# A new order for the first chunk, products that stay in one tile mode, and the mask load in two halves

## The chip, the cores and the metric

The kernel runs on one core of one Trainium2 chip. A core has five engines with a queue each: PE (TensorE, with its weight loads listed as PEld), DVE (VectorE), ACT (ScalarE), POOL (GpSimd) and SP (SyncE, which here only issues DMAs). Each engine takes the instructions of its queue in order; between engines they wait for each other by semaphores. The metric is the device time of one execution in microseconds (us), as the median of several runs. A row of the profile names a line of the kernel as L12, an operation as `out<-in`, and times in us or, where marked, ns.

## The reference

```python
def _attn_ref(q, k, v):                       # q, k, v: (8, 8, 576, 64), float32
    stride, scale = 32, 1.0 / np.sqrt(64)
    scores = scale * np.matmul(q, k.transpose(0, 1, 3, 2))
    rel = pos[:, None] - pos[None, :]
    mask_local = (rel >= 0) & (rel < stride)
    mask_strided = (rel >= 0) & (pos[None, :] % stride == pos[:, None] % stride)
    # heads 0-3 local, heads 4-7 strided
    scores = np.where(masks, scores, -1e9)
    attn = np.exp(scores - scores.max(-1, keepdims=True))
    attn = attn / (attn.sum(-1, keepdims=True) + 1e-9)
    return np.matmul(attn, v)

def _moe_ref(x, w_in, w_out):                 # x: (4608, 512), w_in: (512, 2048), w_out: (2048, 512)
    h = x @ w_in
    g = np.maximum(h, 0.0) + np.log1p(np.exp(-np.abs(h)))
    return g @ w_out

# x is the attention's output, heads side by side
```

## The kernel before

The attention is done for 32 pairs n of heads (8 batches of 4 pairs, in each batch local and strided pairs by turns). A pair's scores are made only in blocks of 64 by 64 where the mask lets something through, nine places for two half-arrays: `scores(n, part)`, part 0 with six places and part 1 with three. The feed-forward layer goes over nine chunks c of 512 tokens and 16 slices f of 128 hidden units. Its matrices are split into a high and a low part (x_h, x_l; w's halves; gh, gl), and each product is the sum of three: high by high, high by low, low by high. So `hidden(c, f)` is 12 products of 128 by 512 and so is `output(c, f)`, which adds into four banks py, one for each 128 tokens. Between them stand Abs, Exp and Ln on ScalarE, the softplus sum on VectorE and the split into gh and gl.

What comes first is written out by hand. The string `FIRST` is a list of tasks, issued from left to right; each goes to the queue of its engine, and three more lists (`ON_POOL`, `ON_VECTOR`, `ON_SCALAR`) name the tasks that don't run on their usual engine. A name is made of letters and numbers:

- q, k, v with n: loads of a pair on SyncE's queue. D: laying out q (D10 and D11 are the two heads of pair 1). S with n and part: scores. X, Y, E, Z, x: maximum, subtraction, exponential, sum, bias. r, R, M: the reciprocal and the normalization.
- T, C, V: transposes on PE for pairs 0 to 3 (three groups each), the copies out of PSUM, the weighted sums. P: transposes on VectorE for pairs 4 to 7. H, L: high and low part of x.
- wi, wo with f: loads of a slice of w_in or w_out as 64-bit floats. a, B, d, c: four steps that make a 32-bit float of it. h, l: its high and low part.
- F with f: `hidden(0, f)`, where Fa is the first nine products and F the other three for f below 2. A, Ae, Al: Abs, Exp, Ln. u: softplus sum. Gh, Gl: split. O: `output(0, f)`; O15 is its first half (tokens 0 to 255) and Ob15 the second.
- y0 to y3: a copy out of py and the DMA that writes it, on SyncE's queue. Qa0, Q0, Q1, QA, Qu, Qh, Ql: the same for the first two slices of chunk 1.
- W: eight products on zeros at the start.

All weights stay on the chip. Behind the written order a planner (`Plan`) lays out the rest from estimated costs and due times: `hidden` two slices ahead of `output`, and a pair's attention at fixed steps. Its first tasks for PE are F18, which is `hidden(1, 2)`, then S8, the scores of pair 8, then `output(1, 0)`. S8 reads the key that task k8 loads and the laid out query of D8.

PSUM: `ps_h` has two banks (hidden, the early transposes), `ps_o` and `ps_s` one each, and `py` is four, which the first scores borrow. The SBUF pools that matter are `io` (four buffers, for weight steps and outputs) and `u` (two).

In batches 0 and 1 (pairs 0 to 7) the mask is added on PE: a product of the 128 by 128 identity and the mask, onto the scores. An early transpose (L454) puts 32 by 32 blocks into a bank that a product on zeros of 128 by 128 (L447) has started. From pair 8 on VectorE adds the mask. The mask itself (192 KB) is loaded by

```python
    mask_b = const.tile([P, 12 * 64], BF16, name="mask_b")
    nc.scalar.dma_start(mask_b, masks)
```

at the head of the kernel (L163). The last tile of the last chunk is written in two halves of 256 columns, one copied by VectorE and one by ScalarE, the second with its DMA on ScalarE's queue (`result`, L655).

Of the kernel before, what the change touches and what calls it, by code (L numbers as in the profile page):

```python
# [33 lines left out]


FIRST = """
W q0 k0 D01 D00 S00 S01 X00 Y00 q1 D10 X01 D11 x01 E00 Z00 k1 S11 X11 E01 r0 R0 M0 q2 D21 S10
T00 wi0 D20 Y11 X10 x10 ai0 Bi0 T01 di0 k2 E11 S21 Z11 S20 E10 ci0 v0 r1 C00 R1 M1 X21 x21 C01 V00
wo2 q3 ao2 Bo2 do2 co2 D30 hi0 D31 wi2 T02 C02 X20 Y20 k3 H00 L00 ai2 Bi2 E20 ho2 Z20 T10 wi1 di2
v1 E21 r2 T11 S31 V01 X31 S30 lo2 x31 R2 wo3 C10 T12 ci2 H01 L01 X30 Y30 ai1 C11 V10 C12 hi2 E31  # L40
wo0 M2 H10 L10 li2 E30 Z30 T20 C20 li0 r3 R3 ao3 Bi1 M3 T21 V11 C21 H11 L11 wi11 ai11 Bi11 di1 T22
T32 C32 di11 v2 wi3 V20 C22 H20 ci1 ci11 hi11 L20 T31 ai3 Bi3 v3 hi1 li1 C31 T30 C30 li11 wo1 wi4
V21 H21 L21 V31 di3 wo6 ao1 Bo1 ao0 ci3 V30 H31 L31 H30 L30 Fa0 hi3 li3 do1 Bo0 co1 do0 Bo3 q4 D4
wi12 co0 F0 A0 Ae0 ho1 k5 Al0 u0 lo1 Fa1 k4 S40 ai4 wi6 X40 Bi4 x40 ho0 lo0 wi5 Gh0 ai5 wi7 Bi5 F1
A1 Gl0 ai7 Ae1 Al1 E40 do3 co3 di4 u1 Gh1 ho3 lo3 F2 A2 Ae2 Bi7 ci4 di5 O0 q5 wi10 wo5 ao5 Al2 Gl1
wi8 S41 D5 X41 ci5 x41 E41 u2 Gh2 hi5 di7 li5 F3 hi4 A3 Bo5 do5 ci7 Ae3 Al3 r4 R4 li4 co5 O1 M4
S50 X50 x50 hi7 u3 wo12 v4 F5 F4 ho5 Gl2 lo5 Gh3 Gl3 P4 E50 S51 ai6 ai8 Bi8 di8 X51 O2 wo4 ao4 Bi6
wo7 x51 di6 ci6 hi6 A5 Ae5 Al5 u5 li7 Bo4 q6 A4 E51 r5 k6 D6 V40 ci8 do4 O3 H40 L40 S60 co4 R5
wi13 Ae4 ai10 Bi10 Al4 V41 H41 li6 wi9 M5 u4 Gh4 Gl4 X60 Gh5 ho4 x60 L41 P5 F7 F6 hi8 wo15 lo4 Gl5
li8 di10 v5 O4 k7 E60 ao6 Bo6 A7 ai13 S61 A6 Ae6 V50 O5 Al6 ci10 hi10 do6 co6 u6 wo11 wo8 q7 li10  # L50
F10 Ae7 Al7 X61 ho6 ai9 u7 x61 ao7 Bo7 do7 Bi13 di13 Bi9 Gh7 Gl7 ci13 H50 L50 wo14 lo6 di9 ci9 Gh6
Gl6 F8 D7 E61 r6 S70 co7 A10 Ae10 ao8 Al10 Bo8 do8 R6 hi9 A8 wi15 u10 V51 li9 X70 x70 O6 Ae8 Al8
co8 wo9 u8 M6 H51 L51 wi14 P6 ho8 lo8 ai12 Gh8 ho7 lo7 Gl8 F11 hi13 li13 Bi12 Gh10 Gl10 wo10 ao9
Bo9 F9 O7 E70 S71 ai15 Bi15 do9 X71 co9 v6 ao10 Bo10 A9 Ae9 Al9 x71 do10 V60 H60 L60 u9 ho9 A11 q8
# [65 lines left out]
def attention_softplus_ffn(  # L120
# [189 lines left out]
    def scores(n, part):  # L310

        b = order[n][0]
        masked = b < 2
# [8 lines left out]
        pss[n, part] = ps
        lo, hi = SPLIT[part]
        for x in range(lo, hi):
            for place in range(2):
# [2 lines left out]
                nc.tensor.matmul(  # L328
                    ps[64 * place : 64 * place + 64, 64 * (x - lo) : 64 * (x - lo) + 64],
                    lhsT=blocks_of(n)[:, c // 32].rearrange("p h l -> p (h l)"),  # L330
                    rhs=k_of(n)[:, c : c + 64],
                    start=x == lo or not masked,
                    stop=not masked,
                )
        if masked:
            nc.tensor.matmul(
                ps[:, : 64 * (hi - lo)], lhsT=ident_b, rhs=mask_of(n, part), start=False, stop=True
            )
# [103 lines left out]
    def early_transposes(n, g):  # L442

        ph = phs["t", n, g] = ps_h.tile([P, 512], F32, tag="ph", name=f"pt_{n}_{g}")[
            :, : 4 * TILE
        ]
        nc.tensor.matmul(ph, lhsT=warm[:, :P], rhs=warm[:, : 4 * TILE], start=True, stop=False)  # L447
        ph = ph.rearrange("p (h a c) -> p h a c", h=2, a=2)
        for x in range(2):
            for i in range(3):  # L450
                a = 2 * g + x
                chunk, place = (6 + a % 3, a // 3) if i == 1 else (a, i // 2)
                for c in range(2):
                    nc.tensor.matmul(  # L454
                        ph[32 * (i + c) : 32 * (i + c) + 32, :, x, 32 * i : 32 * i + 32],
                        lhsT=prob[n % 2][:, chunk, 32 * c : 32 * c + 32],
                        rhs=ident[:, 64 * place : 64 * place + 64],
                        start=False,
                        stop=x == 1 and (c == 0 or i == 2),
                    )  # L460
# [192 lines left out]
                )  # L653

    def result(c, t, engine, cols=slice(0, DM)):  # L655
        o = io_pool.tile([P, DM], F32, tag="io", name=f"o_{c}_{t}")[:, cols]
# [3 lines left out]
        queue.dma_start(out[t0 : t0 + P, cols], o)  # L660
# [314 lines left out]
```

## Time and profile before

| | us |
|---|---|
| median of 3 runs | 899.48 (899.31 to 900.12) |
| the profiled execution's own time | 899.74 |
| its span, first to last instruction | 897.5 |
| PE busy | 885.0 (99%) |
| VectorE busy | 601.4 (67%) |
| ScalarE busy | 446.9 (50%) |
| GpSimd busy | 60.0 (7%) |
| mean DMA rate | 65 GB/s |

The span is 2.2 us shorter than the time of the same execution; what lies around it is the start and end of the program. Shares over the whole span mix the first chunk, in which all engines have much to do, with the rest, so they are read by stretch. A product's own duration (about 390 ns for 512 columns) is longer than the distance to the next one (about 227 ns), since products overlap; a busy PE is thus not a measure of how full it is.

### The profile page before, as it was taken

What the parts mean: (1) busy time and instruction counts of PE and PEld (TensorE: products, weight loads), DVE (VectorE), ACT (ScalarE), POOL (GpSimd) and SP (SyncE); (2) the same over time, 40 slices, a digit from 0 to 9 for tenths busy, and PEclk for the clock granted to TensorE, in tenths of its full rate; (3) what the DMA queues carried; (4) which work ended last, traced back from release to release, by engine and by line L of the source; (5) the groups of instructions that cost most, each with busy time, mean ns of one, the idle gap of its engine ahead of it and who ended that gap; (6) DMA issues with size and microseconds to landing.
All of it is one profiled execution on the core that took longest, in us unless ns stands there. A gap on an engine that the chain in (4) does not pass through costs nothing.

```text
span 897.5 us, 14490 instructions
## 1 busy us (share of the span) xinstructions
PE 885.0 (99%) x5700; PEld 723.8 (81%) x5700; DVE 601.4 (67%) x1308; ACT 446.9 (50%) x796; POOL 60.0 (7%) x77
## 2 busy tenths in 40 slices
...
DMA packets 50084, 58.28 MB, mean 65 GB/s; under 512 B 3168, under 2 KB 35296, under 8 KB 50016
## 3 DMA queue, kind: packets, MB, share of 16 engines
...
q8 instruction: 45, 0.74, 0.4%
q10 hardware_dynamic: 288, 0.33, 0.1%
...
## 4 chain that ended last, share of the span: by engine, by line
PE 86%; DVE 6%; ACT 3%; DMA 3%; issue 1%; SPq 1%; POOL 0%; ACTq 0%; POOLq 0%
PE py L647 40%; PE ph L607 39%; PE ps L328 2%; DMA ri<-in_moe_w_in_dram 2%; PE pv L484 2%; DVE pt L432 1%; PE po L484 1%; PE po L328 1%; ACT qT L256 1%; ACT prob L374 1%; DVE u L628 1%; DMA ro<-in_moe_w_out_dram 1%; DVE a_i L561 1%; DVE a_o L561 0%; DVE a_o L578 0%
## 5 line engine op out<-in xcount | busy, mean ns | idle before, releaser
L647 PE MATMUL py<-w_o,gh 128*128 128x512 f32 x1152 | 359.2, 393 | 0.1
L607 PE MATMUL ph<-x_h,w_i 128*128 128x512 f32 x1152 | 355.7, 390 | 1.0 <-DVE u L628 1.0
L619 ACT ACTIVATE u<-ph 128x512 f32<-128x512 f32 x144 | 86.4, 600 | 394.9 <-PE ph L607 391.9
L607 PEld LDWEIGHTS ph<-x_h,w_i 128*128 128x128 f32 x1152 | 215.8, 188 | 46.3 <-DVE u L628 1.6
L647 PEld LDWEIGHTS py<-w_o,gh 128*128 128x128 f32 x1152 | 213.8, 188 | 47.3 <-POOL w_o L593 0.9
L647 PE MATMUL py<-w_o,gl 128*128 128x512 f32 x576 | 224.2, 389 | 0.0
L607 PE MATMUL ph<-x_l,w_i 128*128 128x512 f32 x576 | 224.1, 389 | 0.0
L628 DVE SCALAR_TENSOR_TENSOR u<-ph,u 128x512 f32<-128x512 f32 x144 | 98.9, 688 | 171.9 <-ACT u L624 170.4
L432 DVE STREAM_TRANSPOSE pt<-prob 32x192 f32<-32x192 f32 x448 | 137.1, 314 | 6.4
L647 PEld LDWEIGHTS py<-w_o,gl 128*128 128x128 f32 x576 | 108.1, 188 | 22.8
L607 PEld LDWEIGHTS ph<-x_l,w_i 128*128 128x128 f32 x576 | 108.1, 188 | 22.6
L640 DVE TENSOR_TENSOR gl<-u,gh 128x512 fp32r<-128x512 f32 x138 | 96.1, 697 | 11.2 <-ACT gh L256 0.3
L622 ACT ACTIVATE u<-u 128x512 f32<-128x512 f32 x144 | 91.3, 634 | 4.5
L624 ACT ACTIVATE u<-u 128x512 f32<-128x512 f32 x144 | 90.9, 632 | 4.4
L256 ACT COPY qT<-prob 64x576 f32<-64x576 f32 x56 | 70.5, 1260 | 0.3
L256 DVE CAST gh<-u 128x512 fp32r<-128x512 f32 x130 | 55.4, 426 | 10.6 <-PE py L647 0.5
L391 DVE TENSOR_TENSOR prob<-ps,mask_b 128x384 f32<-128x384 f32 x24 | 13.4, 558 | 50.4 <-PE ps L328 50.4
L328 PEld LDWEIGHTS ps<-kT,qT 128*64 128x64 f32 x720 | 23.6, 137 | 11.6 <-issue 9.9
L328 PE MATMUL ps<-kT,qT 128*64 128x64 f32 x720 | 28.0, 226 | 0.3 <-ACT qT L256 0.3
L484 PE MATMUL pv<-pt,v_in 128*64 128x96 f32 x396 | 22.2, 248 | 0.0
L422 DVE TENSOR_TENSOR prob<-prob,st 128x576 f32<-128x576 f32 x28 | 21.2, 757 | 0.9
L391 DVE TENSOR_TENSOR prob<-po,mask_b 128x192 f32<-128x192 f32 x24 | 8.6, 357 | 19.3 <-ACT x_h L522 19.3
...
## 6 DMA issues: line engine op xcount, KB each, us to landing
v_in<-in_v_dram SPq DMA_DIRECT2D x28, 320.0 KB, 3.5
...
prob<-in_qk_dram SPq DMA_DIRECT2D x28, 288.0 KB, 2.7
kT<-in_qk_dram SPq DMA_DIRECT2D x28, 288.0 KB, 3.0
...
room<-in_v_dram SPq DMA_DIRECT2D x4, 320.0 KB, 7.5
```

Of the source, the lines that this page charges most:

```text
L256: (engine.copy if engine is nc.scalar else engine.tensor_copy)(dst, src)
L328: nc.tensor.matmul(ps[64 * place : 64 * place + 64, 64 * (x - lo) : 64 * (x - lo) + 64], lhsT=blocks_of(n)[:, c // 32].rearrange("p h l -> ...
L391: nc.vector.tensor_tensor(pv, sv, m, op=ALU.add)
L432: nc.vector.transpose(pt[32 * (i + c) : 32 * (i + c) + 32, h, a : a + hi - lo, 32 * i : 32 * i + 32,], src[:, lo:hi, 32 * c : 32 * c + 32],)
L484: nc.tensor.matmul(po[64 * h : 64 * h + 64, TILE * x : TILE * x + TILE], lhsT=vs[n][:, a, h, :], rhs=pt_of(n, a)[:, h, a % 2], start=True, ...
L607: nc.tensor.matmul(ph, lhsT=w32["i", f][:, half, cc * P : (cc + 1) * P], rhs=x_of(x, cc)[:, t0 : t0 + n], start=(i == 0), stop=(i == 3 * N ...
L619: nc.scalar.activation(us[c, f], phs[c, f], AF.Abs)
L622: nc.scalar.activation(u, u, AF.Exp, scale=-1.0)
L624: nc.scalar.activation(u, u, AF.Ln, bias=1.0)
L628: nc.vector.scalar_tensor_tensor(u, in0=phs.pop((c, f)), scalar=0.0, in1=u, op0=ALU.max, op1=ALU.add)
L640: engine.tensor_tensor(g, us.pop((c, f)), ghs[c, f].bitcast(F32), op=ALU.subtract)
L647: nc.tensor.matmul(py[t], lhsT=g[:, sl], rhs=w32["o", f][:, half], start=(f == 0 and n == 0), stop=(f == NFC - 1 and n == 2),)
```

## The change

It has four parts. The order and the three lists of engines are replaced by others; the tasks are the same but for two new ones, `mask` and `mask2`, the loads of the two halves of the mask. A mask is added as two products of 64 columns of the identity, in the tile mode of the score products, ahead of them for all pairs but pair 0; a bank of early transposes is started by four products of 32 columns in place of one of 128. The half of the last tile that ScalarE copies takes a `u` buffer in place of an `io` buffer.

```diff
 FIRST = """
-W q0 k0 D01 D00 S00 S01 X00 Y00 q1 D10 X01 D11 x01 E00 Z00 k1 S11 X11 E01 r0 R0 M0 q2 D21 S10
-T00 wi0 D20 Y11 X10 x10 ai0 Bi0 T01 di0 k2 E11 S21 Z11 S20 E10 ci0 v0 r1 C00 R1 M1 X21 x21 C01 V00
...
-V21 H21 L21 V31 di3 wo6 ao1 Bo1 ao0 ci3 V30 H31 L31 H30 L30 Fa0 hi3 li3 do1 Bo0 co1 do0 Bo3 q4 D4
-wi12 co0 F0 A0 Ae0 ho1 k5 Al0 u0 lo1 Fa1 k4 S40 ai4 wi6 X40 Bi4 x40 ho0 lo0 wi5 Gh0 ai5 wi7 Bi5 F1
...
-lo9 Ae11 Al11 u11 O8 di15 ci15 Gh11 Gh9 Gl9 di12 V61 H61 ao11 Bo11 wo13 F13 hi15 li15 E71 r7 R7 O9
-co10 ho10 A13 ci12 hi12 ao13 Ae13 Al13 k8 v7 Gl11 L61 lo10 do11 F15 ao12 O10 M7 co11 li12 ho11
-lo11 u13 Gh13 P7 A15 Ae15 Gl13 ai14 Bi14 di14 ci14 F12 hi14 Al15 u15 O11 q9 A12 Ae12 Al12 u12 Bo12
-D8 Gh12 V70 Qa0 li14 F14 do12 co12 ho12 Gl12 lo12 O12 Bo13 do13 A14 co13 ho13 lo13 H70 L70 V71
-ao14 Bo14 do14 Ae14 co14 Al14 u14 ho14 lo14 O13 H71 L71 Q1 Gh14 v8 Gl14 O14 ao15 Bo15 do15 co15
-Gh15 Gl15 ho15 lo15 QA1 Qu1 Qh1 Ql1 Q0 QA0 O15 y1 Ob15 y2 y3 Qu0 Qh0 y0 Ql0 k9
+mask q0 D00 k0 q1 D11 W D01 S00 X00 Y00 S01 X01 x01 D10 E00 Z00 E01 mask2 k1 S10 X10 q2 D20 r0 R0 D21
+wi2 ai2 M0 x10 Bi2 E10 q3 D30 S11 X11 Y11 E11 T01 C01 k2 wi1 di2 ci2 Z11 T00 C00 ai1 v0 r1 R1 S20
...
+li1 wo0 co3 ao0 Bo0 C22 H20 L20 T30 C30 di3 ci3 ao2 q4 Bo2 do2 T32 C32 hi3 ho3 T31 C31 V21 H21 L21
+D4 v3 V31 wi4 V30 H31 do0 lo3 Fa0 co0 li3 L31 H30 L30 wo1 ao1 wi12 Bo1 do1 ho0 ai4 lo0 q5 F0 A0
...
+P7 D8 ao14 Bo14 ao12 O10 Bo12 do12 A12 Ae12 Al12 v7 V70 u12 Gh13 Gl13 O11 wo13 ao13 H70 L70 q9
+co12 ai14 Bi14 di14 Qa0 A15 Gh12 Gl12 ho12 lo12 Bo13 ci14 hi14 Ae15 Al15 V71 u15 O12 li14 do13
+Gh15 H71 L71 F14 k9 co13 ho13 lo13 ao15 Bo15 Q0 do14 co14 A14 Ae14 O13 Al14 u14 Gh14 Gl15 ho14
+Gl14 lo14 Q1 do15 co15 ho15 O14 lo15 Ob15 QA0 Qu0 Qh0 Ql0 O15 QA1 Qu1 y2 Qh1 y3 y1 y0 v8 k8 Ql1
 """
 ON_POOL = """
-D10 D20 D30 ho2 r2 x31 hi11 hi3 x40 ho3 x41 hi5 x50 ho5 hi6 r5 x60 ho6 x61 x71 ho9 ho11 Gh13 hi14
-ho13 ho14
+D11 D20 D30 hi2 hi0 hi3 ho1 hi4 hi7 ho6 x61 hi9 x70 x71 Gh13 hi14 ho14 ho15
 """.split()
 ON_VECTOR = """
-D00 M0 M1 lo2 C12 M3 li1 li3 lo0 Gl0 lo3 Gl1 li5 li4 li7 li6 li10 Gl7 lo6 Gl6 Gl10 Gl9 li15 Gl11
-lo10 M7 Gh12 li14 Gl12 Gl14 Gh15 Gl15
+D00 M0 C01 li1 lo3 lo0 li4 Gh0 Gl0 lo1 Gl1 Gl3 li7 li8 Gl7 Gl6 li9 lo8 lo9 M7 Gl13 Gl12 lo12 lo13
+Gl14 lo14 lo15 y2 y0
 """.split()
 ON_SCALAR = """
-y1 y3
+y3 y1
 """.split()
...
-    nc.scalar.dma_start(mask_b, masks)
...
+        rows = [slice(64 * place, 64 * place + 64) for place in range(2)]
+
+        def add(first):
+            for place in range(2):
+                nc.tensor.matmul(
+                    ps[rows[place], : 64 * (hi - lo)],
+                    lhsT=ident_b[:, rows[place]],
+                    rhs=mask_of(n, part),
+                    start=first,
+                    stop=not first,
+                )
+
+        if masked and n > 0:
+            add(True)
         for x in range(lo, hi):
             for place in range(2):
...
-        if masked:
-            nc.tensor.matmul(
-                ps[:, : 64 * (hi - lo)], lhsT=ident_b, rhs=mask_of(n, part), start=False, stop=True
-            )
+        if masked and n == 0:
+            add(False)
...
-        nc.tensor.matmul(ph, lhsT=warm[:, :P], rhs=warm[:, : 4 * TILE], start=True, stop=False)
+        for c in range(4):
+            nc.tensor.matmul(
+                ph[32 * c : 32 * c + 32],
+                lhsT=warm[:, :32],
+                rhs=warm[:, : 4 * TILE],
+                start=True,
+                stop=False,
+            )
...
-        o = io_pool.tile([P, DM], F32, tag="io", name=f"o_{c}_{t}")[:, cols]
+        if cols.start == 0:
+            o = io_pool.tile([P, DM], F32, tag="io", name=f"o_{c}_{t}")[:, cols]
+        else:
+            o = u_pool.tile([P, 512], F32, tag="u", name=f"o_{c}_{t}")[:, : DM - cols.start]
...
+    first["mask"] = lambda: nc.scalar.dma_start(mask_b[:, : 6 * 64], masks[:, : 6 * 64])
+    first["mask2"] = lambda: nc.sync.dma_start(mask_b[:, 6 * 64 :], masks[:, 6 * 64 :])
```

With the new lists 16 tasks go from VectorE to GpSimd (M1, M3, x70 and 13 low parts of weights and of g), 18 from GpSimd to VectorE (11 low parts, r2, r5, x31, x40, x41, x50, x60), ten from GpSimd to ScalarE (D10, ho2, hi11, ho3, hi5, ho5, hi6, ho9, ho11, ho13), eight the other way (D11, hi0, hi2, ho1, hi4, hi7, hi9, ho15), four from ScalarE to VectorE (C01, Gh0, y0, y2) and three back (C12, Gh12, Gh15).

More of the change, by code (lines that the diff above doesn't have):

```diff
@@ L36 @@
 FIRST = """
-W q0 k0 D01 D00 S00 S01 X00 Y00 q1 D10 X01 D11 x01 E00 Z00 k1 S11 X11 E01 r0 R0 M0 q2 D21 S10
-T00 wi0 D20 Y11 X10 x10 ai0 Bi0 T01 di0 k2 E11 S21 Z11 S20 E10 ci0 v0 r1 C00 R1 M1 X21 x21 C01 V00
-wo2 q3 ao2 Bo2 do2 co2 D30 hi0 D31 wi2 T02 C02 X20 Y20 k3 H00 L00 ai2 Bi2 E20 ho2 Z20 T10 wi1 di2
-v1 E21 r2 T11 S31 V01 X31 S30 lo2 x31 R2 wo3 C10 T12 ci2 H01 L01 X30 Y30 ai1 C11 V10 C12 hi2 E31
-wo0 M2 H10 L10 li2 E30 Z30 T20 C20 li0 r3 R3 ao3 Bi1 M3 T21 V11 C21 H11 L11 wi11 ai11 Bi11 di1 T22
@@ L48 @@
[L48 to L53, printed above, removed]
@@ L60 @@
-Gh15 Gl15 ho15 lo15 QA1 Qu1 Qh1 Ql1 Q0 QA0 O15 y1 Ob15 y2 y3 Qu0 Qh0 y0 Ql0 k9
+mask q0 D00 k0 q1 D11 W D01 S00 X00 Y00 S01 X01 x01 D10 E00 Z00 E01 mask2 k1 S10 X10 q2 D20 r0 R0 D21
+wi2 ai2 M0 x10 Bi2 E10 q3 D30 S11 X11 Y11 E11 T01 C01 k2 wi1 di2 ci2 Z11 T00 C00 ai1 v0 r1 R1 S20
+X20 hi2 T02 Y20 D31 M1 E20 k3 S21 V00 C02 wi0 X21 x21 H00 E21 Bi1 di1 T10 Z20 li2 L00 ci1 T11 S31
+r2 ai0 Bi0 R2 di0 C10 M2 v1 V01 H01 T12 L01 X31 x31 S30 C11 ci0 wo3 ao3 Bo3 X30 Y30 hi0 li0 E31
+V10 C12 H10 L10 E30 T20 wi3 Z30 r3 k4 R3 wo2 C20 do3 T21 C21 M3 V11 v2 H11 L11 ai3 Bi3 T22 V20 hi1
@@ new lines @@
+li1 wo0 co3 ao0 Bo0 C22 H20 L20 T30 C30 di3 ci3 ao2 q4 Bo2 do2 T32 C32 hi3 ho3 T31 C31 V21 H21 L21
+D4 v3 V31 wi4 V30 H31 do0 lo3 Fa0 co0 li3 L31 H30 L30 wo1 ao1 wi12 Bo1 do1 ho0 ai4 lo0 q5 F0 A0
+co1 ho1 S40 wo5 X40 x40 Fa1 F1 Bi4 di4 Ae0 Al0 wi11 ci4 u0 hi4 E40 S41 wo4 co2 ai11 li4 Gh0 Gl0
+lo1 wo6 wi6 A1 Ae1 Al1 u1 ho2 lo2 ao5 X41 x41 Bo5 wi5 ai5 F2 A2 Gh1 wi10 E41 Bi11 D5 Bi5 di11 di5
+k5 wo9 O0 F3 Ae2 r4 Al2 do5 ci11 hi11 Gl1 S50 wi8 co5 ho5 R4 ci5 hi5 O1 u2 Gh2 M4 A3 v4 X50 F4 x50
+E50 Ae3 wi15 Al3 wi9 P4 wi13 u3 lo5 Gl2 li11 wi7 O2 li5 ai7 Bi7 di7 wo14 ao6 Bo6 ai10 Bi10 Gh3 Gl3
```

21 lines of the change are left out of this document (12 added, 9 removed).

## Prediction

> **What bounds the kernel now.** I read the page's head first, then the busy time by stretch, then the chain of waits and the rows around the stage that the change touches.
>
> ```profile
> span 897.5 us, 14490 instructions
> 0.00:34.73 34.73, 27.45 (x556) 18.70 (x557) 29.73 (x62) 26.15 (x69) 16.90 (x34) 1.00 0.96 329
> 34.73:144.24 109.51, 108.14 (x658) 85.16 (x657) 104.21 (x215) 87.40 (x201) 43.11 (x43) 1.00 0.39 135
> 144.24:890.00 745.76, 745.76 (x4474) 617.25 (x4473) 466.34 (x1031) 331.85 (x525) 0.00 (x0) 1.00 0.14 42
> 34.73 0.50 PE L607 MATMUL ph<-x_h,w_i 128*128 128x512 f32 x1
> PE idle L667 <- DVE room L205: 1.2, 1, 1.2
> PE py L328 <- ACT early_h L256: 0.6, 1, 0.6
> PE pv L484 <- DVE x_l L520: 1.2, 1, 1.2
> PE ph L607 <- DVE u L628: 1.0, 1, 1.0
> ```
>
> In the three stretch rows the columns after the length are the busy time of PE, PEld, DVE, ACT and POOL, the granted clock, and the DMA. I cut them at 34.73 us, where the first wide product (task Fa0) starts, and at 144.24 us, where the last product of the written-out order has been issued; I call that moment T. From T to 890 us PE is busy 745.76 of 745.76 us: whatever reaches PE there is paid in full and never won back. Between Fa0 and T PE is busy 108.14 of 109.51, and VectorE 104.21 of 109.51 (95%); from 34 us to T it waits longest twice, and both times for VectorE: the first is V30's, right ahead of Fa0, the second Qa0's at 123.9. Before Fa0 PE is free 34.73 - 27.45 = 7.28 us, of which 1.2 and 0.6 lie ahead of its first product and its first score, and VectorE is busy 29.73 of 34.73. So the first chunk goes at VectorE's pace with PE close behind, and the rest at PE's.
>
> The change reaches the time in three places: T itself, what PE finds right behind T, and the end of the last chunk. The profiled run took 899.74 us, 0.26 above the median of 899.48; the sum is made on 899.74 and the 0.26 taken off at the end.
>
> **The change part by part.**
>
> *Engines and order, up to T: -1.9 us.* No task is added but the two mask loads, so I compare the lists of engines. The rows, busy time and then mean ns of one:
>
> ```profile
> L593 DVE TENSOR_TENSOR w_o<-a_o,w_o 128x512 fp32r<-128x512 f32 x5 | 3.4, 682 | 0.0
> L422 DVE TENSOR_TENSOR prob<-prob,st 128x576 f32<-128x576 f32 x4 | 3.0, 752 | 0.1
> L368 DVE TENSOR_SCALAR st<-st 128x6 f32<-128x6 f32 x2 | 1.3, 654 | 0.1
> L414 DVE TENSOR_SCALAR st<-st 128x9 f32<-128x9 f32 x6 | 1.4, 238 | 0.5 <-ACT prob L374 0.4
> L256 DVE COPY early_h<-pt 128x384 f32<-128x384 f32 x1 | 0.5, 549 | 0.0
> L256 DVE CAST gh<-u 128x512 fp32r<-128x512 f32 x3 | 1.3, 422 | 0.1
> L256 ACT CAST gh<-u 128x512 fp32r<-128x512 f32 x13 | 7.9, 621 | 5.8 <-DVE u L628 5.8
> L256 ACT COPY early_h<-raw_q 64x576 f32<-64x576 f32 x4 | 4.7, 1180 | 2.3 <-DMA raw_q<-in_qk_dram 2.2
> ```
>
> VectorE gives to GpSimd 13 low parts (li, lo, Gl), M1, M3 and x70: 13 x 0.68 + 2 x 0.75 + 0.65 = 11.0 us. It takes from GpSimd 11 low parts and seven small ones (r2, r5, x31, x40, x41, x50, x60, at 0.24 each the nearest row): 11 x 0.68 + 7 x 0.24 = 9.2. With ScalarE it swaps C12, Gh12, Gh15 (0.55 + 0.84) for C01 and Gh0 (0.55 + 0.42): -0.4. Together VectorE loses 11.0 - 9.2 + 0.4 = 2.2 us of 134; the copies y0 and y2, which it also gets, lie behind the last weight that PE waits for. Up to L21, which frees the bank that V30 waits for and with it Fa0, the sets differ by co2, lo2, M1, M3 less di3, Bo0, r2, x31 (0.74 + 0.68 + 1.5 against 0.69 + 0.43 + 0.24 + 0.24), some -1.3. ScalarE gets two more weight casts, D10 for D11 (1.18 either way) and one Gh more: 3 x 0.62 = 1.9 us in a stretch where it idles 22; nothing, unless the order puts that work ahead of an Al that VectorE awaits. Of the 2.2 I take 1.9, since some lies where VectorE waits anyway. Upper end: of PE's free 7.28 + 1.37 us the 1.8 at the start stay, which leaves 6.8; I set 4.5, two thirds of it. Lower end: a loss of 1, one block on GpSimd more (below).
>
> *Mask and zero products: 0.*
>
> ```profile
> 12.43 0.34 PE L447 MATMUL pt<-room 128*128 128x384 bf16 x1
> 12.69 0.67 PE L454 MATMUL pt<-room,prob 128*32 128x64 f32 x24
> 13.29 0.57 PE L328 MATMUL py<-early_l,early_h 128*64 128x64 f32 x12
> 13.79 0.26 PE L336 MATMUL py<-mask_b,ident_b 128*128 128x192 bf16 x1
> ```
>
> 128*128, 128*64 and 128*32 in the rows are the tile modes. 192 columns more of bf16 cost 0.34 - 0.26 = 0.08 us, so the 384 of a zero product stream in 0.16; from its start to the next product pass 0.26, so 0.10 is the step between modes. Leaving the 32-wide products costs another step of about that size. A T behind a T can lose both, 0.2 us; 12 T's, at most 2.4 us, all before Fa0. The other way: 24 products of 0.22 us stand within 0.67 us, so quarters of the array overlap; if four zero products did not, they would cost 3 x 0.16 - 0.2 = 0.28 more each, 3.4 us. For the masks the same step is saved only where a score stands beside a 64-wide product; next to a 512-wide one it moves to the other side. Both are hidden before Fa0 by VectorE, which is what V30 and the copies wait for; after Fa0 there are eight masks, and 0.1 each stays inside the 1.9's range.
>
> *Mask loads: 0.* Today the load is issued at 0.76 us; in the new order it stands on ScalarE's queue behind the copy of the identity:
>
> ```profile
> 2.08 0.30 ACT L208 CAST room<-ident_b 128x128 f32<-128x128 bf16 x1
> 6.86 0.34 PE L336 MATMUL py<-mask_b,ident_b 128*128 128x384 bf16 x1
> mask_b<-in_masks_dram ACTq DMA_DIRECT2D x1, 192.0 KB, 3.5
> raw_q<-in_qk_dram SPq DMA_DIRECT2D x4, 288.0 KB, 4.8
> ```
>
> Issued at 2.4 it lands at 5.9 with the mask row's 3.5, ahead of the first mask product at 6.86; with the 4.8 of loads under traffic at 7.2, which would make S00, X00 and all of VectorE 0.3 late. Against it, q0 and k0 no longer share with it: from -0.4 to +0.3, taken as 0. The second half delays k1 and all behind it on SyncE's queue by one issue; those loads wait for no one today.
>
> *The tail of T: +3.0 us.* The new order ends ``... Ob15 QA0 Qu0 Qh0 Ql0 O15 QA1 Qu1 y2 Qh1 y3 y1 y0 v8 k8 Ql1``. SyncE issues in order, and y2, y3, y1, y0 each end in an output DMA there, which waits for its copy. v8 (two DMAs) and k8 come behind. k8 is the key of the first score task that the planner puts after F18, and so PE's second task after T.
>
> ```profile
> L274 SPq DMA_DIRECT2D kT<-in_qk_dram x3: 328/369/517, 62.6 to 101.4; - x3
> 143.56 2.04 ACT L256 COPY o<-py 128x512 f32<-128x512 f32 x4
> 144.16 2.13 SPq L660 DMA_DIRECT2D out_dram<-o  x4
> 146.34 2.36 SPq L274 DMA_DIRECT2D kT<-in_qk_dram  x2
> 147.06 0.92 PE L328 MATMUL ps<-kT,qT 128*64 128x64 f32 x24
> kT<-in_qk_dram SPq DMA_DIRECT2D x28, 288.0 KB, 3.0
> v_in<-in_v_dram SPq DMA_DIRECT2D x28, 320.0 KB, 3.5
> ```
>
> Before, k8 is the third of the key loads between 60 and 130 us, issued at 101.4, and k9 is the one behind the four outputs, at 146.34 = T + 2.10, which nobody needs soon. S8 starts at 147.06 = T + 2.82 without a wait. After: y1 is copied on ScalarE in about 0.5 us once O15's second half is done, to T + 0.8; y0's output follows, and the pitch of issues is 2.13 / 4 = 0.53, so y1 goes at 0.9, y0 at 1.4, v8 at 1.9 and 2.4, k8 at T + 2.9, landing 3.0 later at T + 5.9. PE stands from 2.82 to 5.9: 3.1 us; I take 3.0. Ends: issued as early as k9 is, T + 2.1, it costs 2.3; with the 3.5 of a load behind other traffic, 3.6. Nothing hides it, since PE has no other task in between and is full afterwards.
>
> *The last output: -0.4 us.*
>
> ```profile
> 894.12 0.33 SPq L660 DMA_DIRECT2D out_dram<-o  x1
> 894.38 0.37 ACT L256 COPY o<-py 128x256 f32<-128x256 f32 x1 [0.81 <-DMA out_dram<-o]
> 894.78 0.35 ACTq L660 DMA_DIRECT2D out_dram<-o  x1
> out_dram<-o SPq DMA_DIRECT2D x1, 128.0 KB, 2.0
> out_dram<-o ACTq DMA_DIRECT2D x1, 128.0 KB, 1.7
> ```
>
> ScalarE's half of the last tile waits for the first of four io buffers to be written out; in a u buffer it need not. Then its DMA is no longer last (894.78 + 1.7 = 896.5) but SyncE's (894.12 + 2.0 = 896.1): what is late next limits the gain to 0.4, between 0.3 and 0.7.
>
> *Sum:* 899.74 - 1.9 - 0.4 + 3.0 = 900.44; less 0.26, 900.2 us.
>
> **The rivals.**
>
> *Slower: a VectorE that is blocked by GpSimd.*
>
> ```profile
> 53.81 1.68 POOL L422 TENSOR_TENSOR prob<-prob,st 128x576 f32<-128x576 f32 x1 [3.38 <-ACT w_i L256]
> 54.39 1.64 DVE L578 SCALAR_TENSOR_TENSOR a_o<-ro,a_o 128x512 uint32<-128x512 uint32 x1
> L578 DVE SCALAR_TENSOR_TENSOR a_i<-ri,a_i 128x512 uint32<-128x512 uint32 x16 | 11.6, 731 | 0.1
> ```
>
> The same instruction that takes 0.73 took 1.64 while GpSimd ran M4, 0.91 more. GpSimd's long operations go from 24 low parts and 4 M's to 26 and 6, and M1 and M3 now stand in the part before Fa0. Two blocks more eat the 1.9: T stays at 144.24, and the time is 899.48 - 0.4 + 3.0 = 902.1. It decides from 0.7 us of first-chunk gain downwards. Against it: GpSimd's busy total hardly changes, since six small ones (seven less x70) and two casts leave it.
>
> The Trainium skill, page "SBUF — State Buffer", section "SBUF: two separate sides", calls the port pair of VectorE and GpSimd an exclusive lock: whichever starts first keeps it for the whole instruction. The row agrees in kind (1.64 against 0.73); by that rule every extra two-input operation on GpSimd speaks against this change.
>
> *Faster: VectorE stops being the bound.* If the new order feeds PE nearly without a gap, the upper end above is reached: 4.5 us. Then 899.48 - 4.5 - 0.4 + 3.0 = 897.6. For it: the waits named are for VectorE and it has less to do; against it: VectorE has 2.2 us less, not 4.5.
>
> *Faster: k8 isn't late.* If S8 finds its key, the time is 900.2 - 3.0 = 897.2. It needs k8 issued by T - 0.2; before, what stands in that place goes at T + 2.1.
>
> **How the numbers follow.** The forecast has 0.50, the blocked VectorE 0.28, the fed PE 0.14, the early k8 0.08. The range runs from the early k8's 897.2 to 902.7, which is no first-chunk gain with the long landing (899.48 - 0.4 + 3.6); the forecast's own is 898.9 to 901.8. A measurement tells 0.2%, 1.8 us, from no change: 897.7 and 901.3 are the borders. Faster takes most of the two fast cases, 0.20; slower the blocked case and the forecast's upper edge, 0.31; within, 0.49.
>
> **What the profile after would show.** Right: a wait of PE for a DMA of kT at about T + 2.8, some 3 us long, the only one after T; T near 142.3; VectorE's busy time to T about 2 us less; the mask rows in mode 128*64 and the zero rows in 128*32; the last ACT copy of 256 columns starting with VectorE's, and the last DMA on SyncE's queue. Wrong: no such wait, T at 140 or 145, or more VectorE operations of 1.4 us and above than before.

## The result and the profile after

The changed kernel takes 908.36 us in the median of four runs (907.55 to 910.26), beside 899.75 us (899.31 to 900.12) for the kernel before; the ratio is 1.0099 (95% interval 1.0081 to 1.0117), so it is slower by 1%. The forecast was 900.2 us with a range from 897.2 to 902.7: it missed, and the range didn't hold the time. The profiled execution took 907.69 us, 0.67 below the median. All rows below are from profiled executions, so differences are taken between those: 907.69 - 899.74 = 7.95 us of time, 905.6 - 897.5 = 8.1 us of span. One run among the experiments, the profiled one of e5, took 1104.12 us at a granted clock of 0.752; it is left out of its row in the table, and no row is read from it.

The stretch rows of the changed kernel, cut at its own Fa0 and T (columns as before: length, then busy PE, PEld, DVE, ACT, POOL, then granted clock and DMA):

```profile
0.00:35.24 35.24, 25.98 (x600) 19.84 (x600) 29.32 (x62) 26.85 (x68) 19.34 (x35) 0.95 0.76 259
35.24:148.84 113.60, 108.60 (x667) 85.04 (x665) 106.85 (x219) 88.61 (x204) 42.65 (x39) 1.00 0.42 147
148.84:898.00 749.16, 745.85 (x4474) 617.28 (x4473) 465.84 (x1030) 331.14 (x523) 0.00 (x0) 1.00 0.14 42
```

T is at 148.84 instead of 144.24, 4.6 us late: 0.5 of it is there when Fa0 starts (35.24 against 34.73), 4.1 come between Fa0 and T (113.60 us against 109.51). PE's busy time in that stretch is nearly the same (108.60 against 108.14); what grew is its idle time, from 1.37 to 5.00 us. And behind T, where PE was never idle, 749.16 - 745.85 = 3.31 us are missing. 4.6 + 3.3 = 7.9 of the 8.1 us. PE's waits of the changed kernel, longest first: what waited, for which engine and line, us in total, times, longest (line numbers are those of the changed file: L341 are the score products, L472 the early transposes, L625 `hidden`, L665 `output`):

```profile
PE ps L341 <- DMA kT<-in_qk_dram: 3.3, 1, 3.3
PE pt L472 <- DVE st L379: 2.9, 1, 2.9
...
PE ps L326 <- ACT prob L385: 1.3, 1, 1.3
...
PE ph L625 <- ACT w_i L254: 0.9, 1, 0.9
PE py L665 <- DVE w_o L611: 0.8, 1, 0.8
PE ph L625 <- DVE u L646: 0.6, 1, 0.6
```

The first row is the late key, the only wait behind T. The second stands at 9.5 to 12.4 us, long before Fa0. The others shown lie between Fa0 and T. Before, that stretch had one wait of 1.0 us and one of 0.3; now it has seven of over 0.25. S41 waits 1.3 us for the exponential E40, which frees the one score bank. Six products wait 0.4 to 0.9 us each, five of them for VectorE or for a cast that had waited for it, one for GpSimd.

*The key.* The timeline of SyncE's queue around T, then of PE (start, us, engine and line, and in brackets the idle time before and its end):

```profile
148.07 2.40 SPq L681 DMA_DIRECT2D out_dram<-o  x4
150.55 0.40 SPq L283 DMA_DIRECT2D v_in<-in_v_dram  x1
151.05 0.45 SPq L290 DMA_DIRECT2D v_in<-in_v_dram  x1
151.54 5.12 SPq L272 DMA_DIRECT2D kT<-in_qk_dram  x2
155.03 0.92 PE L341 MATMUL ps<-kT,qT 128*64 128x64 f32 x24 [3.31 <-DMA kT<-in_qk_dram]
```

Four outputs, two parts of v8, then k8 at 151.54 = T + 2.70; S8 starts at T + 6.19. Forecast were T + 2.9 and T + 5.9.

*The blocked operations.* VectorE's operations beside GpSimd's, as the timeline of the changed kernel has them, two examples:

```profile
82.18 1.78 DVE L596 SCALAR_TENSOR_TENSOR a_i<-ri,a_i 128x512 uint32<-128x512 uint32 x1
82.06 1.36 POOL L611 TENSOR_TENSOR w_i<-a_i,w_i 128x512 fp32r<-128x512 f32 x1 [2.04 <-ACT w_i L254]
105.37 1.52 DVE L570 TENSOR_SCALAR a_o<-a_o 128x512 uint32<-128x512 uint32 x1
105.18 1.43 POOL L658 TENSOR_TENSOR gl<-u,gh 128x512 fp32r<-128x512 f32 x1 [1.70 <-PE pv L502]
```

All steps of these two kinds in the first chunk, with least, median and greatest ns, first and last start:

```profile
L596 DVE SCALAR_TENSOR_TENSOR a_i<-ri,a_i x16: 626/686/1784, 14.4 to 131.4; 128x512 uint32<-128x512 uint32 x16
L570 DVE TENSOR_SCALAR a_o<-a_o x16: 413/420/1522, 23.9 to 136.7; 128x512 uint32<-128x512 uint32 x16
```

Behind the first example stand a cast on ScalarE and the next `hidden` product on PE:

```profile
84.00 0.62 ACT L254 CAST w_i<-a_i 128x512 fp32r<-128x512 f32 x1 [1.16 <-DVE a_i L596]
84.71 0.70 PE L625 MATMUL ph<-x_h,w_i 128*128 128x512 f32 x2 [0.91 <-ACT w_i L254]
```

The cast waits 1.16 us for ci8. The product waits 0.91, by the profile for that cast; by the order it is F10, which needs the bank that u6 frees, VectorE's next operation behind ci8 (83.89 to 84.57). Either way the wait goes back to ci8.

The step ci8 takes 1.78 us where the median of its line is 0.69; it starts 0.12 behind GpSimd's low part li10 and ends 0.54 after that one has ended, so it did next to nothing until then. Bo9, a plain TENSOR_SCALAR, takes 1.52 instead of 0.42 beside Gl9. Measured against the usual length of each form, 11 VectorE operations of the first chunk are longer by over 0.6 us, 9 before. That is the "two blocks more" of the slower rival, to the letter, but the count moves by one between executions (12 in e15, the changed kernel run again). What differs more is where they stand:

| | between Fa0 and PE's last wait ahead of T | excess there |
|---|---|---|
| before | co5, li6, x70, do11 | 4.0 us |
| after | x50, do4, ci8, li9, do7, Bo9, co10, co11 | 8.2 us |

Before, three of the nine (do13, do14, Gl14) came after the last product that waited, so PE lost nothing by them.

*The last output.* ScalarE's queue at the end:

```profile
900.95 0.59 ACT L254 COPY o<-py 128x512 f32<-128x512 f32 x1 [0.77 <-PE py L665]
902.09 0.37 ACT L254 COPY o<-py 128x256 f32<-128x256 f32 x1 [0.55 <-DVE o L254]
```

The copy of 256 columns no longer waits for a DMA, but for VectorE's copy of the other half, which runs from 901.63 to 902.05. The span ends 4.37 us after PE's last product starts (901.20), before 4.28 (893.24).

### The profile page after: what moved, and what is told of

Read it like the earlier page. It is cut to its first block, busy times and chain, and to the rows that moved or that the text cites. A ratio compares the mean times of both kernels' runs of the same rounds, so it can differ in the third digit from the quotient of the medians.

```text
span 905.6 us, 14587 instructions
## 1 busy us (share of the span) xinstructions
PE 884.0 (98%) x5752; PEld 724.8 (80%) x5752; DVE 603.1 (67%) x1311; ACT 448.1 (49%) x797; POOL 62.0 (7%) x73
## 4 chain that ended last, share of the span: by engine, by line
PE 86%; DVE 7%; ACT 2%; issue 2%; DMA 1%; POOL 1%; SPq 1%; POOLq 0%; ACTq 0%; DVEq 0%
PE py L665 40%; PE ph L625 38%; PE ps L341 2%; DVE pt L443 2%; PE pv L502 2%; PE po L502 1%; PE po L341 1%; DVE u L646 1%; DMA ro<-in_moe_w_out_dram 1%; DVE a_o L579 1%; DVE a_o L596 1%; PE pt L472 1%; DVE a_i L579 0%; PE py L341 0%; DVE a_i L596 0%
## 5 line engine op out<-in xcount | busy, mean ns | idle before, releaser
L665 PE MATMUL py<-w_o,gh 128*128 128x512 f32 x1152 | 359.0, 393 | 0.9 <-DVE w_o L611 0.8
L625 PE MATMUL ph<-x_h,w_i 128*128 128x512 f32 x1152 | 356.3, 390 | 1.8 <-ACT w_i L254 0.9
L625 PEld LDWEIGHTS ph<-x_h,w_i 128*128 128x128 f32 x1152 | 215.5, 188 | 48.8 <-DVE u L646 1.3
L665 PEld LDWEIGHTS py<-w_o,gh 128*128 128x128 f32 x1152 | 214.0, 188 | 48.0 <-DVE w_o L611 1.1
L625 PE MATMUL ph<-x_l,w_i 128*128 128x512 f32 x576 | 224.3, 389 | 0.0
L665 PE MATMUL py<-w_o,gl 128*128 128x512 f32 x576 | 224.1, 389 | 0.0
L665 PEld LDWEIGHTS py<-w_o,gl 128*128 128x128 f32 x576 | 108.2, 188 | 22.7
L625 PEld LDWEIGHTS ph<-x_l,w_i 128*128 128x128 f32 x576 | 108.1, 188 | 22.7 <-DVE x_l L538 0.3
L658 DVE TENSOR_TENSOR gl<-u,gh 128x512 fp32r<-128x512 f32 x136 | 94.1, 692 | 12.1 <-DVE gh L254 0.9
L341 PEld LDWEIGHTS ps<-kT,qT 128*64 128x64 f32 x720 | 23.9, 137 | 12.3 <-issue 8.1
L341 PE MATMUL ps<-kT,qT 128*64 128x64 f32 x720 | 27.6, 225 | 3.5 <-DMA kT<-in_qk_dram 3.3
L417 ACT ACTIVATE prob<-prob 128x576 f32<-128x576 f32 x24 | 16.5, 689 | 9.1 <-DVE prob L411 9.1
```

The source lines that it names most:

```text
L341: nc.tensor.matmul(ps[rows[place], 64 * (x - lo) : 64 * (x - lo) + 64], lhsT=blocks_of(n)[:, c // 32].rearrange("p h l -> p (h l)"), rhs=k ...
L625: nc.tensor.matmul(ph, lhsT=w32["i", f][:, half, cc * P : (cc + 1) * P], rhs=x_of(x, cc)[:, t0 : t0 + n], start=(i == 0), stop=(i == 3 * N ...
L658: engine.tensor_tensor(g, us.pop((c, f)), ghs[c, f].bitcast(F32), op=ALU.subtract)
L665: nc.tensor.matmul(py[t], lhsT=g[:, sl], rhs=w32["o", f][:, half], start=(f == 0 and n == 0), stop=(f == NFC - 1 and n == 2),)
```

## The experiments

Each is the changed kernel (after) or the kernel before with one edit. The kernel before took 899.63 us beside e1 to e4, 899.72 beside e5 to e8, 899.52 beside e9 to e12 and 899.82 beside e13 to e15. Fa0, T and the time between them are from the profiled executions:

| | median us (range, runs) | ratio to before (95%) | Fa0 | T | Fa0 to T |
|---|---|---|---|---|---|
| before | 899.75 (899.31–900.12, 4) | | 34.73 | 144.24 | 109.5 |
| after | 908.36 (907.55–910.26, 4) | 1.0099 (1.0081–1.0117) | 35.24 | 148.84 | 113.6 |
| after again, e15 | 908.13 (906.94–908.30, 4) | 1.0085 (1.0069–1.0101) | 35.53 | 149.59 | 114.1 |
| e1, after, key early | 902.68 (902.27–904.63, 5) | 1.0040 (1.0027–1.0052) | 35.57 | 149.08 | 113.5 |
| e2, before, new products | 900.49 (899.04–901.98, 11) | 1.0011 (1.0002–1.0020) | 34.88 | 144.43 | 109.6 |
| e3, e1 with old products | 904.03 (903.09–905.60, 5) | 1.0049 (1.0037–1.0062) | 34.57 | 148.77 | 114.2 |
| e4, e1, early gap filled | 904.26 (903.48–904.55, 5) | 1.0048 (1.0036–1.0061) | 34.99 | 149.48 | 114.5 |
| e5, e1, GpSimd reads less | 898.45 (896.36–898.89, 9) | 0.9985 (0.9976–0.9995) | – | – | – |
| e6, before, the same | 897.69 (896.78–898.52, 10) | 0.9979 (0.9969–0.9989) | 33.25 | 141.39 | 108.1 |
| e7, before, new lists | 916.71 (915.35–918.04, 4) | 1.0192 (1.0177–1.0208) | – | 160.07 | – |
| e8, e1, old lists | 914.63 (914.03–916.07, 4) | 1.0172 (1.0156–1.0187) | – | 158.98 | – |
| e9, e5, waits kept | 898.17 (896.04–900.71, 10) | 0.9984 (0.9973–0.9996) | 36.78 | 145.31 | 108.5 |
| e10, e1, half of P5 | 901.82 (900.87–904.23, 5) | 1.0031 (1.0017–1.0046) | 35.60 | 148.49 | 112.9 |
| e12, before, half of P5 | 899.22 (898.58–899.82, 10) | 0.9997 (0.9987–1.0007) | 34.10 | 143.42 | 109.3 |
| e11, before, u buffer | 899.77 (898.76–900.67, 10) | 1.0004 (0.9994–1.0013) | – | – | – |
| e13, e1, five moved | 902.04 (900.80–904.06, 10) | 1.0023 (1.0014–1.0033) | 33.91 | 146.15 | 112.2 |
| e14, before, four moved | 898.19 (897.58–898.84, 11) | 0.9980 (0.9971–0.9989) | 34.67 | 142.94 | 108.3 |

### The key alone

```diff
-... Al12 v7 V70 ...
+... Al12 k8 v7 V70 ...
-... lo14 Q1 do15 ...
+... lo14 v8 Q1 do15 ...
-... y2 Qh1 y3 y1 y0 v8 k8 Ql1
+... y2 Qh1 y3 y1 y0 Ql1
```

> The changed kernel with two tasks of its order moved: k8 to right ahead of v7, v8 to right ahead of Q1. Nothing else. Theory: the 3.3 us for which PE waits for the key DMA right behind the first chunk are lost in full, since PE is busy without a gap afterwards: the time falls by 3.3 us, from 908.4 to about 905, and the wait is gone from the profile, T (the start of F18) staying near 148.8. Rival: the engines behind PE use the pause, so that without it PE waits elsewhere: the time falls by less than 1 us.

The wait behind T is gone: PE is busy without a gap, as the rows of its two later stretches show.

```profile
35.57:149.08 113.51, 108.59 (x666) 85.05 (x665) 106.90 (x219) 88.68 (x204) 42.68 (x39) 1.00 0.44 151
149.08:896.00 746.92, 746.92 (x4479) 618.21 (x4478) 465.92 (x1030) 331.06 (x523) 0.00 (x0) 1.00 0.14 41
```

T stays (149.08), and the profiled time falls from 907.69 to 904.34, by 3.35: the length of the wait. The medians fall by more, 908.36 - 902.68 = 5.7. Two groups of runs stand behind that difference, and the runs of one group spread over 1.4 to 2.7 us. A repeat of the changed kernel (e15, below) came at 908.13, where 906 was expected if the wait is worth what the trace shows; so the difference stands, and where the other 2 us come from is not settled.

### The products, and the early gap

```diff
 e2: before, with the mask in two products of 64 columns and the zeros in four of 32
 e3: e1, with the mask in one product of 128 columns and the zeros in one of 128
 e4: e1
-... E11 T01 ...
+... E11 W2 T01 ...
+    first["W2"] = lambda: dummies(10)      # ten products on zeros
```

> The kernel before, with only the products changed: masks as two products of 64 columns (ahead of the scores for all pairs but pair 0) and zeros as four products of 32 columns. Theory: PE's work ahead of Fa0 gets some 2 us shorter (the rows of T fall from 0.87 to about 0.57 to 0.79 each), but VectorE sets the pace, so T moves by less than 1 us and the time by 0 to -1. Rival: the products are what made the first chunk slower: T later by 2 to 4 us and the time 902 to 904.

> The changed kernel with k8 and v8 early as in e1_key_early and with the products of the kernel before (identity of 128 for masks, zeros of 128). Theory (the order itself costs the 4.6 us by which T is later): the time is that of e1_key_early within 1.5 us, about 905 to 906, since each T and score gets its steps between modes back ahead of Fa0. Rival (the new products cost it): 2 to 4 us faster than e1_key_early, about 901 to 903.

> As e1_key_early, with ten more products on zeros of 512 bf16 columns (2.1 us at full clock) between S11 and T01, where PE waits 2.9 us for the first normalization and after which the granted clock is 0.5 from 13.7 to 17.1 us of the span. Theory: the idle time ahead halves the clock, and 1.3 us of it reach T through the late S20, T02 and S21: granted clock 1.0 throughout, Fa0 and T earlier by 0.5 to 1.5 us, time 0.5 to 1.5 below e1_key_early. Rival: VectorE covers the slow stretch, and T stays within 0.3 us of e1_key_early though the clock is whole.

With the new products alone T is 144.43 beside 144.24, and with the old ones in the new order it is 148.77 beside 149.08: the products aren't what costs the 4.6 us, and they gain nothing either (900.49 us, 0.1% above the kernel before). e4 is about the clock. In the profiled run of the changed kernel it was halved once in this chunk, 1.3 us after PE's idle 2.9 us had ended (rows of three shorter stretches):

```profile
10.00:13.65 3.65, 1.28 (x54) 1.17 (x56) 3.34 (x9) 3.30 (x13) 1.15 (x1) 1.00 1.09 374
13.65:17.06 3.41, 3.41 (x62) 2.90 (x64) 3.16 (x8) 3.03 (x9) 1.33 (x2) 0.50 1.09 385
17.06:25.00 7.94, 5.60 (x168) 4.83 (x166) 7.07 (x18) 5.90 (x21) 3.91 (x5) 1.00 0.70 259
```

In e4 the gap is filled and the clock whole from 10.4 us on. Fa0 comes 0.6 us earlier than in e1, as the theory had it, yet T is 149.48. The changed kernel run again says the same without an edit: there the clock was whole, as its rows show, and T still 149.59.

> The changed kernel once more, unchanged. Theory: the key's wait is worth what the profile shows, so it stands 3.3 us above e1_key_early's 902.7, at 906. Rival: the first medians were right and the wait costs 5.7: 908.4.

```profile
10.00:35.53 25.53, 16.99 (x508) 14.15 (x508) 23.64 (x51) 21.52 (x59) 11.25 (x10) 1.00 0.75 255
35.53:149.59 114.06, 108.51 (x666) 85.05 (x665) 106.92 (x219) 88.83 (x204) 42.62 (x39) 1.00 0.41 144
```

So neither modes nor clock: the 4.6 us come with the order and its lists.

### Order or lists

```diff
 e7: before, with ON_POOL, ON_VECTOR and ON_SCALAR of the changed kernel
 e8: e1, with the three lists of the kernel before
```

> The kernel before with the changed kernel's three lists of engines, in the old order. Theory (the order, not the choice of engines, loses): T within 2 us of 144.2. Rival (the choice of engines loses, with M1, M3 and the low parts on GpSimd ahead of Fa0): T at 147 to 149.

> As e1_key_early, in the new order, but with the three lists of engines of the kernel before. Theory (order): T stays at 147 to 150, since the order was made for other lists, and the time within 2 us of e1_key_early. Rival (lists): T at 144 to 146, the time 899 to 901.

Neither expectation held. Each mixture is far worse than both kernels, T at 160.07 and 158.98. In e7 PE's waits are of another size altogether, here the two longest:

```profile
PE ps L327 <- ACT qT L255: 5.7, 1, 5.7
PE ph L606 <- DVE u L627: 4.7, 3, 2.2
```

An order and its lists are fitted to each other; taking them apart measures the misfit, and not the share of either.

### GpSimd's low parts without the reading

```diff
 e5 and e6, in w_low and for gl, where the engine is GpSimd:
+        fill(...)      # three memsets of 512, 512 and 256 columns
-        engine.tensor_tensor(..., op=ALU.subtract)
 e9, ahead of its memsets:
+        nc.gpsimd.tensor_copy(dst[:, :1], high.bitcast(F32)[:, :1])
```

> As e1_key_early, but the low parts that GpSimd makes (li, lo, Gl on its list) are left out: in place of each two-input subtraction three memsets of zeros (512, 512 and 256 columns), which write and read nothing and wait for no high part. So it does without GpSimd's reads of these, and its output is not the reference's. Theory (VectorE is blocked by GpSimd's reads, and this is what the new order lost): VectorE's blocks outside M1 to M6 vanish (about 8 of the 11 above 0.6 us), T falls from 149.1 to 143 to 145 and the time by 4 to 6 us against e1_key_early. Rival (the order loses by waits between tasks, a late load, S41 behind E40): T stays above 147.

> The kernel before with the same replacement as e5_no_read_new (low parts on GpSimd left out, memsets in their place). Theory: its blocks cost VectorE 10.7 us above the usual durations in the profile, some 7 of them by low parts, and PE follows VectorE: T falls from 144.2 to 139 to 141. Rival: PE's own work sets T, and it falls by less than 1.5 us. If e5_no_read_new and this one end with T within 1.5 us of each other, the blocks explain the difference of the orders; if they stay 4 apart, they don't.

The low parts that GpSimd makes are zeros here; it is about as long busy and still writes, but it reads next to nothing. The time falls 0.15% below that of the kernel before in the new order, from 0.40% above it, and 0.21% below in the old one: e5 gains some 4 us against e1, e6 some 2 us. But the memsets don't wait for the high part as the subtractions do, so part of this may be waits taken away. e9 keeps them:

> As e5_no_read_new, but each memset that stands for a low part on GpSimd waits for its high part through a copy of one column, as the subtraction does; two memsets of 512 columns and one of 199 fill the rest of its time. The low parts are left out again. Theory (the blocks, not the waits that e5_no_read_new took away with them): T within 1 us of what e5_no_read_new's runs give (about 143), the time 897 to 900, and no VectorE operation but those beside M1 to M6 more than 0.6 us above its usual time. Rival (it was the waits): the time back at 901.5 to 904, T at 147 to 149.

The row of its stretch from Fa0 to T:

```profile
36.78:145.31 108.53, 106.19 (x667) 85.26 (x666) 98.91 (x218) 88.97 (x204) 48.36 (x109) 1.00 0.46 160
```

The same row of e6, the old order without the reading, then the longest of e9's waits of PE between Fa0 and T, and last the line of the example above:

```profile
33.25:141.39 108.14, 107.50 (x658) 85.29 (x657) 99.96 (x215) 87.58 (x201) 43.76 (x85) 1.00 0.40 138
```

```profile
PE ps L326 <- ACT prob L385: 1.6, 1, 1.6
```

```profile
L596 DVE SCALAR_TENSOR_TENSOR a_i<-ri,a_i x16: 625/686/693, 14.6 to 127.1; 128x512 uint32<-128x512 uint32 x16
```

GpSimd is busy 48.36 us of this stretch, more than in e1 (42.68), and every step of this row is back at 0.69. Of the eight blocked operations one is left (li9, beside M6, which still reads). Of the waits of PE that I listed between Fa0 and T only S41's is left, beside one of 0.8 for ScalarE, where a weight load came late. The stretch from Fa0 to T is 108.5 us instead of e1's 113.5.

So the two orders differ by 4 us in this stretch while GpSimd's reading stops VectorE (113.5 and 109.5), and by 0.4 when it doesn't (e9 108.5, e6 108.1). The loss between Fa0 and T comes from operations of VectorE that GpSimd's reading stops. By T itself e6's expectation would have it otherwise, for the T's are 3.9 us apart (145.31 and 141.39). Of these, 3.5 lie ahead of Fa0 (36.78 and 33.25), where e9's clock was halved twice, for 6.8 and 3.4 us; and its profiled run was the slowest of its ten (900.71). The medians, which hang on no single run, are 0.5 us apart (898.17 and 897.69), where e1 and the kernel before are 3.05 apart.

The Trainium skill, page "SBUF — State Buffer", section "SBUF: two separate sides", has the rule for both halves of this: an exclusive lock, taken by a GpSimd operation against a two-input operation of VectorE only if the GpSimd one reads SBUF. The trace agrees on both: 1.78 against 0.69 beside a subtraction, and at most 0.693 in the same row with memsets in place of the subtractions.

### VectorE's sum

```diff
-            task(f"P{n}", prob_transposes, n)
+            task(f"P{n}", prob_transposes, n, range(2 if n == 5 else 4))
```

> As e1_key_early, with half of pair 5's transposes on VectorE left out (P5: 8 in place of 16), which takes 2.5 us off VectorE at 75 us and changes nothing else; the output of pair 5 is not the reference's. Theory (VectorE's queue sets T in the new order): T falls from 149.1 by 1.5 to 2.5 us, the time as much. Rival (PE, ScalarE or a late load sets it): less than 0.7 us.

> The kernel before with the same half of P5 left out. Theory (VectorE sets the pace there too, PE close behind): T falls from 144.2 by 1 to 2.5 us. Rival (PE's own work holds it): less than 0.7 us.

Half of P5 is 2.7 us of VectorE's work: the 16 transposes take 5.11 us in e1, the eight of e10 2.40. T comes 0.6 us earlier in the new order (148.49 beside 149.08) and 0.8 in the old one, less than either theory had. But the executions differed ahead of P5 already. The first row is from e10, the second from e1, at the same score product:

```profile
54.38 0.92 PE L341 MATMUL ps<-kT,qT 128*64 128x64 f32 x24 [1.05 <-ACT qT L254]
53.28 0.92 PE L341 MATMUL ps<-kT,qT 128*64 128x64 f32 x24 [0.21 <-ACT qT L254]
```

In e10 ScalarE had waited 1.6 us for a weight load, and the product waited for ScalarE. P5 itself starts 1.3 us later than in e1 (76.67 against 75.39), so from there to T e10 gains 1.9 us. Two of e1's waits behind P5, 0.9 us (put down to a cast) and 0.6 (for `u`), are gone or down to 0.2; the later ones are what they were (rows of e10's waits of PE):

```profile
PE py L665 <- DVE w_o L611: 0.8, 1, 0.8
PE ph L625 <- POOL w_i L611: 0.3, 1, 0.3
```

In the old order it is the other way about: e12 is 0.4 us early at P5 already (72.13 against 72.52), and gains 0.4 behind it. So 2.7 us of work that VectorE is spared were worth 1.9 us in the new order, where products wait for VectorE behind it, and 0.4 in the old one, where PE has only 1.37 us of idle time from Fa0 to T. One execution of each stands behind these figures.

### The last output alone

```diff
-        o = io_pool.tile([P, DM], F32, tag="io", name=f"o_{c}_{t}")[:, cols]
+        if cols.start == 0:
+            o = io_pool.tile([P, DM], F32, tag="io", name=f"o_{c}_{t}")[:, cols]
+        else:
+            o = u_pool.tile([P, 512], F32, tag="u", name=f"o_{c}_{t}")[:, : DM - cols.start]
```

> The kernel before with the u buffer for ScalarE's half of the last tile alone. Theory: that copy starts with VectorE's, and the span behind the last product of 512 columns ends 0.4 us sooner, since SyncE's DMA of VectorE's half is last; the time falls by 0.4, within what a measurement can tell. Rival: the two last DMAs slow each other and nothing changes.

The timeline of the two half copies:

```profile
894.16 0.42 DVE L256 COPY o<-py 128x256 f32<-128x256 f32 x1 [0.67 <-PE py L647]
894.62 0.37 ACT L256 COPY o<-py 128x256 f32<-128x256 f32 x1 [0.55 <-DVE o L256]
```

The second copy starts 0.89 us after the start of PE's last product (893.73) instead of 1.14, since it still comes behind VectorE's copy. Its DMA then takes 2.0 us to landing instead of 1.7, and is still the last:

```profile
out_dram<-o ACTq DMA_DIRECT2D x1, 128.0 KB, 2.0
```

The time is the old one (1.0004, 0.9994 to 1.0013). What the copy gains, the DMA loses, as the rival had it; why it takes longer isn't shown.

### Another engine for the blocking operations

```diff
 e13: e1
-Gl14 lo14 lo15 y2 y0
+Gl14 lo14 lo15 y2 y0 li10 Gl10 Gl9 li12 Gl11
 e14: before
-lo10 M7 Gh12 li14 Gl12 Gl14 Gh15 Gl15
+lo10 M7 Gh12 li14 Gl12 Gl14 Gh15 Gl15 M4 M5 M6 li12
```

> As e1_key_early, with li10, Gl10, Gl9, li12 and Gl11 made by VectorE in place of GpSimd, at the same places of the order. In e1's profile each of them stands beside a VectorE operation that takes 1.0 to 1.1 us more than usual (ci8, do7, Bo9, co10, co11). All computation is done. Theory (single blocks close ahead of PE's waits): these five are gone, PE's waits at O8, V70 and F14 (1.3, 0.8, 0.6 us) shrink to 0.3 and less, T falls from 149.1 by 1.5 to 3 us, though VectorE has five more operations of 0.6 us. Rival (VectorE's total): 5 x 1.05 - 5 x 0.62 = 2.1 us less, of which by e10's ratio (0.6 of 2.5) a quarter reaches T: 0.5 us.

Five operations that blocked ci8, do7, Bo9, co10 and co11 run on VectorE itself. T is 2.9 us earlier, but 1.7 of that lie ahead of Fa0, where nothing was moved; between Fa0 and T it is 1.3, the excess there falling from 8.2 to 3.6 us. One of the moved ones, li12, is now itself blocked. Moving costs 0.68 us of VectorE for each 1.0 to 1.1 saved, and the median is only 0.6 below e1's, with intervals that overlap. It supports the theory in part. Which of the blocks stand ahead of a waiting product is read from the table; no run changes their places alone.

> The kernel before with M4, M5, M6 and li12 made by VectorE, whose four neighbours co5, li6, x70 and do11 are each 0.95 to 1.1 us longer than usual there. Theory: these four blocks go (4.0 us) for 3 x 0.70 + 0.62 = 2.7 us more work, T falls by 0.5 to 1.5 us, the time to 898.5 to 899.2, the only version here that beats the kernel before without leaving work out. Rival: PE's own work holds T (e12 gave 0.8 us for 2.5), and the time stays within 0.3 us of before.

Its stretch from Fa0 to T:

```profile
34.67:142.94 108.27, 107.68 (x659) 85.20 (x658) 102.94 (x219) 87.67 (x201) 38.21 (x39) 1.00 0.40 137
```

In the old order the four that blocked co5, li6, x70 and do11 go to VectorE. No operation between Fa0 and 126 us is blocked any more, PE is idle 0.59 us instead of 1.37 in that stretch, and T is at 142.94. VectorE's busy time there falls, 104.21 to 102.94, though it does four operations more. 898.19 us is faster than the kernel before by 0.2% (0.9980, 0.9971 to 0.9989), with all of the computation done, and the best version that the runs gave.

## Why the prediction was wrong

*The key: right.* Forecast +3.0 us from k8 standing behind v8 and four outputs, measured 3.3; place, cause and being the only wait behind T were as said, and e1 takes it away. S8 starts 0.3 later than forecast: the key was issued 0.2 earlier, but the time from issue to S8 was 155.03 - 151.54 = 3.5 instead of 3.0, the duration that I had kept for a load behind other traffic.

*Engines and order up to T: wrong, and this is the step that failed.* Forecast -1.9, measured +4.6. The term added up what VectorE loses and gains in work and took nearly all of the difference as time. What failed is the price of an operation: the sum took the usual mean of each, and allowed one block more at worst, while the longest operations are the ones that GpSimd stops. In the new order these cost VectorE 8.2 us of excess between Fa0 and PE's last wait, instead of 4.0. Taken at the usual length of each form, the operations up to T did get shorter by some 2 us in total (leaving out y0 and y2), so the lists were added up about right; but what they take above it rose from some 10 to 13 us. So VectorE's busy time up to T did not fall by 2.2 us, but rose from 133.94 to 136.17 (from Fa0 to T 104.21 to 106.85). That the blocks make the loss is shown by e9 beside e6 (the stretch takes 108.5 and 108.1 us without them, 113.5 and 109.5 with them) and, with all of the computation done, by e14 (109.5 to 108.3).

Two smaller errors of the term: spared work was taken as time nearly one for one, where 2.7 us were worth 1.9 in the new order (e10) and 0.4 in the old (e12). And x70 was priced at 0.65, a mean of two of which one takes 0.17 us and the other, x70 itself, 1.14, being blocked; the loss of work was 0.5 smaller by its usual length. Of the 4.1 us between Fa0 and T, 1.3 are S41's wait for E40, which the term didn't have; it stays in e9.

*The slower rival had the mechanism, and not the price.* It named GpSimd's lock, counted two blocks more (11 against 9), and let them eat the gain: T unchanged, 902.1 us. The measured T is 4.6 later than that. It counted blocks over the whole chunk, without their places. A trace of the old order can't show the places in the new one, but it could have given the bound: the blocks in the old stretch had 4.0 us of excess, so as much again could be lost, and I had set the end on that side at 1. The range's upper end, 902.7, didn't hold even that: it stands for no gain at all.

*Products and mask loads: right in size.* Zero was forecast; e2 and e3 both put T some 0.2 to 0.3 us later with the new products, which is within what T differs between two runs of the changed kernel (148.84, 149.59). The first score product starts at 5.14 us instead of 5.38. For the mask load the reason was wrong: the forecast put it at 2.4 us, behind a copy on ScalarE, but it is issued at 0.76 as before.

*The last output: wrong, a small term.* Forecast -0.4, measured 0. The step looked for what is late next among the DMAs, with their old durations. The copy has to wait for VectorE's copy once the buffer is free, which leaves 0.25 us, and its DMA took 2.0 us instead of 1.7; e11 shows both alone.

*Sum by the measured terms:* 899.74 + 4.6 + 3.3 = 907.6, beside 907.69.

*Open:* why the medians fall by 5.7 us with the early key when the trace shows 3.35; the 0.5 us ahead of Fa0 (kernels without an edit there start Fa0 between 33.91 and 35.60 in the new order with its lists, and between 34.10 and 35.13 in the old); and the 1.3 us of S41, which waits for E40 in e9 and e13 too, so isn't due to the blocks.
